# Closing a full expert in the gate logits on ScalarE, and making the repeated search keys on ScalarE alone

## The chip, the core and the metric

The kernel runs on one core of one Trainium2 chip. The metric is the device time of one execution in microseconds (us). Before the change the median of three runs is 2402.73 us (2402.56 to 2403.67).

## The reference: squared-ReLU attention, then experts filled greedily to capacity

```python
scores = scale * np.matmul(z, z.transpose(0, 2, 1))     # z: 8 x 2496 x 64
attn = np.maximum(scores, 0.0) ** 2
x = (u * np.matmul(attn, v)).reshape(B * S, D)          # 19968 x 256
logits = x @ w_gate                                     # 8 experts
for idx in np.argsort(-logits.flatten()):               # best logit first
    tok, e = idx // E, idx % E
    if assigned[tok] >= 0 or counts[e] >= cap:          # cap = 19968 / 8 = 2496
        continue
    assigned[tok] = e
    counts[e] += 1
for e in range(E):                                      # every expert on its 2496 tokens
    out[assigned == e] = np.maximum(x[assigned == e] @ w1[e], 0.0) @ w2[e]
```

A token goes to its best expert that still has room. An expert that is full is out of the race, and its remaining tokens go to their next best.

## The kernel before

The attention fills the first 1,360 us or so and isn't touched. After it, `moe` runs the experts one after the other, in the order in which they become full: k = 0 to 7. The tokens of an expert are worked on in five groups g of 512 (the last has 448), and each group in eight steps f. A step is 14 or so matmuls on TensorE (PE): six in `expand` (L664 to L666, into one of two PSUM buffers `hp`), and eight in `contract` (L757 and L760, for a step three earlier). Between them stand ScalarE's ReLU, which writes `hh` (L742), and VectorE's low half of the product, `hl_` (L744). For the last group VectorE also writes a piece of `hh` (L747), which is the last to read `hp`. A buffer `hp` is filled again only when ReLU, L744 and L747 have read it. VectorE also adds the outputs `y` (L784), splits weights (`w1l`, L613, behind ScalarE's `w1h`, L610) and turns gathered tokens (`tr`, L644).

While PE works on expert k-1, the generator `route(k)` finds the tokens of the next one. Its work is cut into pieces by `yield`, and `advance` hands out so many pieces per step. So the code's order mixes the two, and a scheduler at build time sets the final order on each engine from it; each engine then runs its own list in order. For k = 1 to 7 `route(k)` does this:

- It closes the expert that was filled last: `closed` (128 x 8) is a large negative number in its column and zero elsewhere, and is added to the logits `lg` (128 partitions x 160 tokens x 8 experts) on VectorE in two halves (L343). `closed` shares its memory with `rab`, which the one-hot rows of the expert before still read, so that it comes behind the last of them.
- `best_steps` (L81 to L98) finds each token's best expert and its logit `m`, in two halves.
- `order_keys` turns `m` into integer keys, and `spread` repeats their upper 16 bits eight times side by side in `rep` (L136 on ScalarE for the first half of the tokens, L137 on VectorE for the second).
- Two stages of six search rounds follow. A round compares `rep` with up to seven thresholds (`mask`, L128), counts on PE (L288, L399) and picks the next thresholds (L404, L408). Between the stages `spread` fills `rep` again, from `near`. The last expert needs no search.
- At the end it ranks the tokens (`tot`, L458 and L470, and what follows), makes one-hot rows `ob` in eight large instructions (L515), and PE turns these in four blocks (L521) into the list `idx` (L526), from which GpSimd gathers the tokens (L582).

The expert k = 0 has its own code and nothing of it changes.

Of the kernel before, what the change touches and what calls it, by code (L numbers as in the profile page):

```python
# [14 lines left out]
AF = mybir.ActivationFunctionType  # L15
# [60 lines left out]
def best_steps(nc, first, c, eq):  # L76
    lg, m, code, oh = [first[n][:, c] for n in ("lg", "m", "code", "oh")]
    shape = list(lg.shape)
    E = shape[2]
    cb = first["code8b"][:, None, :].to_broadcast(shape)  # L80
    nc.vector.tensor_reduce(m, lg, axis=AX.X, op=OP.max)  # L81
    yield
    nc.vector.tensor_tensor(eq, lg, m[:, :, None].to_broadcast(shape), op=OP.is_ge)
    yield
    nc.vector.tensor_mul(eq, eq, cb)
    yield
    if shape[1] < E:
        nc.vector.tensor_reduce(code, eq, axis=AX.X, op=OP.max)
        yield
        nc.vector.tensor_tensor(oh, code[:, :, None].to_broadcast(shape), cb, op=OP.is_equal)  # L90
        return
    nc.vector.tensor_max(eq[:, :, :4], eq[:, :, :4], eq[:, :, 4:])
    yield
    nc.vector.tensor_max(eq[:, :, :2], eq[:, :, :2], eq[:, :, 2:4])
    yield
    nc.vector.tensor_max(code, eq[:, :, 0], eq[:, :, 1])
    yield
    nc.vector.tensor_tensor(oh, code[:, :, None].to_broadcast(shape), cb, op=OP.is_equal)  # L98


def order_keys(nc, first, c, alone=False):
    for _ in key_steps(nc, first, c, alone):
        pass


def key_steps(nc, first, c, alone):
    m, sign, key, rep, top, low = [first[n][:, c] for n in ("m", "sign", "key", "rep", "top", "low")]
    m = m.bitcast(I32)
    nc.vector.tensor_scalar(sign, m, 31, 0x7FFFFFFF, op0=OP.arith_shift_right, op1=OP.bitwise_and)
    yield  # L110
    nc.vector.scalar_tensor_tensor(key, m, 0x8000, sign, op0=OP.bitwise_xor, op1=OP.bitwise_xor)
    yield
    half = key.bitcast(I16).rearrange("p (j h) -> p j h", h=2)
    spread(nc, rep, half[:, :, 1], alone)
    yield
    if half.shape[1] == first["key"].shape[1]:
        nc.scalar.activation(top, half[:, :, 1], AF.Copy, scale=65536.0)
        nc.scalar.activation(low, half[:, :, 0], AF.Copy)
        return
    nc.vector.tensor_scalar(top, half[:, :, 1], 65536.0, None, op0=OP.mult)  # L120
    yield
    nc.vector.tensor_copy(low, half[:, :, 0])


def at_least(nc, mask, x, T, lo, hi):
    for a in range(0, T.shape[1], 8):
        z = min(T.shape[1], a + 8)
        nc.vector.tensor_tensor(mask[:, lo:hi, a:z], x[:, lo:hi, :z - a],  # L128
                                T[:, None, a:z].to_broadcast([128, hi - lo, z - a]), op=OP.is_ge)


def spread(nc, rep, x, alone=False):
    n = x.shape[1]
    h = 0 if alone else n // 2
    if h:
        nc.scalar.activation(rep[:, :h], x[:, :h, None].to_broadcast([128, h, 8]), AF.Copy)  # L136
    nc.vector.tensor_copy(rep[:, h:], x[:, h:, None].to_broadcast([128, n - h, 8]))  # L137


def moe(tc, xd, first, jp, identf, w1, w2, out, B, S, cp, dram):  # L140
    nc = tc.nc
    E, D, F = w1.shape
# [7 lines left out]
    lg, m, code, oh, code8, code8b, xr = [first[n] for n in ("lg", "m", "code", "oh", "code8", "code8b", "rep")]  # L150
    JP = lg.shape[1]
# [14 lines left out]
    with ExitStack() as ctx:  # L166
# [109 lines left out]
        def srch():  # L276
            return ps.tile([128, 512], F32, name="srch", bufs=1)
# [56 lines left out]
        def behind(lag):  # L334
            return tc.issue_after(paced[-lag].ins) if len(paced) >= lag else nullcontext()

        def route(k):
            if k:
                closed = rp.tile([128, E], F32, name="closed", tag="rab")
                nc.vector.tensor_scalar(closed, ROUTE[k - 1]["star"], SHUT, None, op0=OP.mult)  # L340
                for c in range(0, JP, JP // 2):
                    o = lg[:, c:c + JP // 2]
                    nc.vector.tensor_add(o, o, closed[:, None, :].to_broadcast([128, JP // 2, E]))  # L343
                    yield 0.7
                for c in range(0, JP, JP // 2):
                    eq = rp.tile([128, JP // 2, E], BF, name="eq")
                    for i, _ in enumerate(best_steps(nc, first, slice(c, c + JP // 2), eq)):
                        if i == 2:
                            yield 6.8 / 4
                    yield 6.8 / 4  # L350
                done = rp.tile([128, JP], F32, name="done")
                with behind(1):
                    nc.vector.tensor_scalar(done, asg, 0.0, GONE, op0=OP.is_gt, op1=OP.mult)
                nc.vector.tensor_add(m, m, done)
                order_keys(nc, first, slice(0, JP))
                yield 1.5
# [13 lines left out]
            else:  # L370
# [7 lines left out]
                for stage in range(2):  # L378
                    for r, w in enumerate(widths):
                        n = (1 << w) - 1  # L380
                        if r == 0:
                            T = first["at0"] if k == stage == 0 else at0
                        else:
                            T = rp.tile([128, ND + 1], I16, name="T", bufs=2)[:, :n + 1]
                            nc.vector.tensor_tensor(T, step[:, r, :n + 1], V.to_broadcast([128, n + 1]), op=OP.add)
                        whole = first["mask0"] if n > 7 else rp.tile([128, JP, n], BF, name="mask")
                        cuts = [0, JP] if k else [JP - 16, JP] if T is first["at0"] else [0, JP // 2, JP]
                        for lo, hi in zip(cuts, cuts[1:]):
                            at_least(nc, whole, xr, T[:, :n], lo, hi)
                        yield 2  # L390
                        if k:
                            x = hist(lambda j: whole[:, j, :n], n, "jt")
                        else:
                            p, o = quad_hist(lambda j: whole[:, j, :n], n, r)
                        warm(k, 4)
                        yield 2.2
                        if k:
                            o = srch()[:, :E * (n + 1)]
                            nc.tensor.matmul(o, onesr, x, start=True, stop=True)  # L399
                        else:  # L400
                            quad_sums(p, o, n, "jt")
                        warm(k, 10 if r + 1 < len(widths) or stage else 30)
                        best = rp.tile([128, E, ND + 1], F32, name="best")[:, :, :n + 1]
                        nc.vector.scalar_tensor_tensor(best, o.rearrange("p (e t) -> p e t", e=E), 0.0,  # L404
                                                       T[:, None].to_broadcast([128, E, n + 1]),
                                                       op0=OP.min, op1=OP.add)
                        V = rp.tile([128, 1], F32, name="V", bufs=3)
                        nc.vector.tensor_reduce(V, best, axis=AX.XY, op=OP.max)  # L408
                    tstar = V
                    if stage == 0:  # L410
                        base = rp.tile([128, 1], F32, name="base")
                        nc.vector.tensor_scalar(base, tstar, 65536.0, None, op0=OP.mult)
                        rel = rp.tile([128, JP], F32, name="rel")
                        nc.vector.scalar_tensor_tensor(rel, first["top"], base, first["low"],
                                                       op0=OP.subtract, op1=OP.add)
                        near = rp.tile([128, JP], I16, name="near")
                        nc.vector.tensor_scalar(near, rel, 32767.0, -32768.0, op0=OP.min, op1=OP.max)
                        spread(nc, xr, near)
                        yield 1.5
                T = tstar  # L420
                g = rp.tile([128, 2, JP], BF, name="fmask")
# [4 lines left out]
                if k:  # L426
                    x = hist(lambda j: g[:, :, j], 2, "tj")
                    yield
                    o = srch()[:, :E * 2]
                    nc.tensor.matmul(o, onesr, x, start=True, stop=True)  # L430
                else:
                    p, o = quad_hist(lambda j: g[:, :, j], 2, 1)
# [3 lines left out]
                o = o.rearrange("p (e t) -> p e t", t=2)  # L436
# [63 lines left out]
            if k:  # L500
                p = srch()
                for c in range(0, JP, CB):
# [16 lines left out]
                    for j in range(c, min(J, c + CB)):  # L519
                        n, r = divmod(j - c, QW)  # L520
# [16 lines left out]
            for a0, a1 in ((0, 8), (8, 2 * KT)):  # L537
                na = a1 - a0
                p = srch()
                for c in range(0, JP, CB):  # L540
# [13 lines left out]
                    for j in range(c, min(J, c + CB)):  # L554
                        n, r = divmod(j - c, QW)
# [746 lines left out]
```

## Time and profile before

| what | value |
|---|---|
| median of the runs | 2402.73 us |
| the profiled execution: time | 2405.74 us |
| its span, first to last instruction | 2403.9 us |
| PE busy | 2367.9 us, 99% |
| VectorE (DVE) busy | 2026.1 us, 84% |
| ScalarE (ACT) busy | 1531.9 us, 64% |
| GpSimd (POOL) busy | 474.9 us, 20% |
| mean granted clock of PE | 0.995 |

Shares of the whole span say little about a single stage: VectorE is idle for a sixth of the span, and yet there are stretches in which it never stops. The time of the profiled execution lies 1.84 us over its span and 3.0 us over the median of the runs.

### The profile page before, as it was taken

How to read it: one execution, taken by the hardware profiler on the slowest of the kernel's cores; microseconds unless marked ns; L12 is line 12 of the kernel's file. 1: busy time of each engine (PE TensorE's matmuls, PEld its weight loads, DVE VectorE, ACT ScalarE, POOL GpSimd, SP SyncE). 2: the span in 40 equal slices, each digit the busy share in tenths (PEclk: the TensorE clock that was granted, in tenths of full speed). 3: DMA queues.
4: the chain of work that ended last, by engine and by line, in shares of the span. 5: the costliest groups of instructions: out<-in, count | busy, mean ns of one | idle time of the engine just before them, and what ended most of it. 6: DMA issues, size and time to landing. Idle time of an engine off the chain costs nothing.

```text
span 2403.9 us, 42413 instructions
## 1 busy us (share of the span) xinstructions
PE 2367.9 (99%) x14724; PEld 1985.2 (83%) x14724; DVE 2026.1 (84%) x5887; ACT 1531.9 (64%) x2932; POOL 474.9 (20%) x693
## 2 busy tenths in 40 slices
PE   8999999999999999999999999999999999999998
PEld 6888888888888888888888777788888888888887
DVE  7899898998999998999989888979797979797443
ACT  7898888988889888898888413424342434244332
POOL 3010020020010100200200013324333334344332
PEclk9999999999999999999999899999999999999999
DMA  4254262262262351622512112334342424243331
GB/s 150 49 134 102 53 157 53 58 178 50 52 161 53 83 145 34 160 75 54 138 27 53 27 54 80 110 84 123 82 123 81 128 79 132 78 141 105 101 98 54
DMA packets 233847, 222.27 MB, mean 92 GB/s; under 512 B 95392, under 2 KB 192672, under 8 KB 233504
## 3 DMA queue, kind: packets, MB, share of 16 engines
q1 hardware_dynamic: 193088, 150.58, 23.3%
q0 software_dynamic: 40544, 68.98, 10.5%
q8 instruction: 116, 1.90, 0.3%
q14 instruction: 99, 0.81, 0.1%
HBM read 158.67 MB, written 60.82 MB: 91 GB/s over the span
## 4 chain that ended last, share of the span: by engine, by line
PE 83%; issue 8%; DVE 4%; POOL 3%; DMA 1%; ACT 1%; POOLq 0%; DVEq 0%; SPq 0%; ACTq 0%
PE acc L1029 41%; PE sc L987 11%; PE y L757 8%; PE hp L664 4%; PE hp L665 4%; PE hp L666 4%; PE y L760 4%; POOL xg L582 2%; PE acc L1034 1%; PE srch L288 1%; POOL out_dram L792 1%; PE srch L521 1%; DMA zr<-in_z_dram 1%; PE xp L330 1%; DVE mask L128 1%
## 5 line engine op out<-in xcount | busy, mean ns | idle before, releaser
L1016 DVE TENSOR_TENSOR lo<-r,hi 128x512 fp32r<-128x512 f32 (+1 forms) x800 | 536.7, 674 | 82.1 <-ACT hi L1008 78.8
L1029 PE MATMUL acc<-hi,vh 128*128 128x512 f32 (+1 forms) x1520 | 591.3, 389 | 0.8 <-ACT vh L961 0.8
L1029 PE MATMUL acc<-lo,vh 128*128 128x512 f32 (+1 forms) x1520 | 588.2, 387 | 2.7 <-DVE lo L1016 2.7
L1029 PE MATMUL acc<-hi,vl 128*128 128x512 f32 (+1 forms) x1520 | 586.4, 386 | 0.0
L1008 ACT ACTIVATE hi<-r 128x512 fp32r<-128x512 f32 (+1 forms) x780 | 500.4, 642 | 122.3 <-ACT r L1003 86.1
L742 ACT ACTIVATE hh<-hp 128x512 fp32r<-128x512 f32 (+1 forms) x319 | 187.1, 587 | 557.0 <-PE hp L666 482.9
L1003 ACT ACTIVATE r<-r 128x512 f32<-128x512 f32 (+1 forms) x800 | 504.0, 640 | 2.5 <-DVE r L997 2.4
L1070 DVE SCALAR_TENSOR_TENSOR lt<-xs,wgb 128x256 bf16<-128x256 f32 x1192 | 449.7, 418 | 0.6 <-DMA xs<-xd 0.4
L757 PE MATMUL y<-w,hh 128*128 128x512 f32 x1280 | 367.1, 398 | 0.2 <-DVE y L784 0.2
L1029 PEld LDWEIGHTS acc<-hi,vh 128*128 128x128 f32 x1520 | 286.3, 188 | 67.0 <-issue 13.8
L999 ACT ACTIVATE r<-sc 128x512 f32<-128x512 f32 (+1 forms) x638 | 312.4, 617 | 40.2 <-PE sc L987 39.7
L1029 PEld LDWEIGHTS acc<-lo,vh 128*128 128x128 f32 x1520 | 286.5, 188 | 59.2 <-DVE lo L1016 8.5
L1029 PEld LDWEIGHTS acc<-hi,vl 128*128 128x128 f32 x1520 | 286.5, 188 | 51.9 <-DVE vl L971 0.2
L582 POOL DMA_INDIRECT xg<-xd,idx x160 | 186.8, 1168 | 465.0 <-DVE xg L620 269.0
L757 PEld LDWEIGHTS y<-w,hh 128*128 128x128 f32 x1280 | 235.5, 189 | 45.1 <-DVE y L784 1.3
L664 PE MATMUL hp<-xh,w1h 128*128 128x512 f32 (+2 forms) x642 | 255.9, 400 | 3.9 <-DVE hh L747 2.4
L665 PE MATMUL hp<-xl,w1h 128*128 128x512 f32 (+2 forms) x642 | 251.4, 392 | 0.6 <-DVE xl L658 0.5
L666 PE MATMUL hp<-xh,w1l 128*128 128x512 f32 (+2 forms) x642 | 249.8, 389 | 0.0
L987 PE MATMUL sc<-z,z 64*128 64x512 f32 (+1 forms) x1920 | 235.9, 388 | 5.3 <-ACT z L952 2.7
L987 PEld LDWEIGHTS sc<-z,z 64*128 64x128 f32 x1920 | 202.6, 185 | 29.6 <-ACT z L952 3.4
L792 POOL DMA_INDIRECT out_dram<-y,idx x160 | 169.0, 1056 | 215.0 <-DVE y L784 126.2
L950 POOL DMA_DIRECT2D z<-in_z_dram x35 | 18.7, 534 | 960.3 <-DVE lt L1070 639.6
(1192 smaller groups left out, 2880.9 us busy)
## 6 DMA issues: line engine op xcount, KB each, us to landing
ur<-in_u_dram SPq DMA_DIRECT2D x39, 512.0 KB, 4.6
flat<-tr SPq DMA_DIRECT2D x152, 128.0 KB, 2.8
xt<-flat SPq DMA_DIRECT2D x38, 512.0 KB, 3.6
vh<-in_v_dram POOLq DMA_DIRECT2D x133, 128.0 KB, 4.6
vr<-in_v_dram SPq DMA_DIRECT2D x32, 512.0 KB, 4.3
xd<-tr SPq DMA_DIRECT2D x128, 128.0 KB, 3.0
xs<-xd SPq DMA_DIRECT2D x32, 512.0 KB, 4.4
wr<-in_moe_w_dram SPq DMA_DIRECT2D x32, 512.0 KB, 5.9
```

The costliest lines, as they stand in the source:

```text
L582: return nc.gpsimd.indirect_dma_start(out=dst, out_offset=None, in_=src, in_offset=bass.IndirectOffsetOnAxis(ap=idx, axis=0))
L664: nc.tensor.matmul(p[:, c], wh, xh, start=(d == 0), stop=False)
L665: nc.tensor.matmul(p[:, c], wh, xl, start=False, stop=False)
L666: latest["mm"] = nc.tensor.matmul(p[:, c], wl, xh, start=False, stop=(d == DH - 1))
L757: nc.tensor.matmul(o, h[:, c], w.rearrange("p s d -> p (s d)"), start=(f == 0), stop=(f == FT - 1), skip_group_check=True)
L987: nc.tensor.matmul(pair[s], key[b, p][r, c * 128:c * 128 + 128], query[b, g][r, :w], start=key is ZH and query is ZH, stop=key is ZL)
L999: recent["r"] = nc.scalar.activation(r, p, AF.Relu, scale=scale)
L1003: nc.scalar.activation(R[n], R[n], AF.Square)
L1008: nc.scalar.activation(h, R[n], AF.Copy)
L1016: recent["l"] = nc.vector.tensor_sub(LO[n], a, h.bitcast(F32))
L1029: nc.tensor.matmul(o[d], w[:, c[d]], x, start=(kt == 0 and i == 0), stop=False)
L1070: nc.vector.scalar_tensor_tensor(t[r], src[r], 1.0, WG["rows"][r, e], op0=OP.mult, op1=OP.mult, accum_out=lg[r, j, e:e + 1])
```

## The change

For a full expert, ScalarE now adds `closed` to the logits, in eight instructions, one for each expert's column, each with that column of `closed` as its bias (`AF.Identity`). The two pieces that `advance` counted for it at 0.7 are now one of 1.4. And where `spread` filled half of `rep` on each engine, ScalarE fills all of it for the keys of k = 1 to 7 and for `near` of k = 1 to 6; VectorE's half goes away. The first expert, and the partial calls inside the attention, stay as they were.

```diff
     half = key.bitcast(I16).rearrange("p (j h) -> p j h", h=2)
-    spread(nc, rep, half[:, :, 1], alone)
+    n = half.shape[1]
+    spread(nc, rep, half[:, :, 1], 0 if alone else n if n == first["key"].shape[1] else n // 2)
     yield
-    if half.shape[1] == first["key"].shape[1]:
+    if n == first["key"].shape[1]:
...
-def spread(nc, rep, x, alone=False):
+def spread(nc, rep, x, h):
     n = x.shape[1]
-    h = 0 if alone else n // 2
     if h:
         nc.scalar.activation(rep[:, :h], x[:, :h, None].to_broadcast([128, h, 8]), AF.Copy)
-    nc.vector.tensor_copy(rep[:, h:], x[:, h:, None].to_broadcast([128, n - h, 8]))
+    if h < n:
+        nc.vector.tensor_copy(rep[:, h:], x[:, h:, None].to_broadcast([128, n - h, 8]))
...
                 nc.vector.tensor_scalar(closed, ROUTE[k - 1]["star"], SHUT, None, op0=OP.mult)
-                for c in range(0, JP, JP // 2):
-                    o = lg[:, c:c + JP // 2]
-                    nc.vector.tensor_add(o, o, closed[:, None, :].to_broadcast([128, JP // 2, E]))
-                    yield 0.7
+                for e in range(E):
+                    nc.scalar.activation(lg[:, :, e], lg[:, :, e], AF.Identity, bias=closed[:, e:e + 1])
+                yield 1.4
...
-                        spread(nc, xr, near)
+                        spread(nc, xr, near, JP if k else JP // 2)
```

The change also moves what it doesn't name. The lists of the engines are the same until the end of the first expert's routing; from there on the routing work stands at other places among the steps. Three places matter, all in the routing of the second expert (k = 1) and the start of the third's. In the rows the numbers behind a name tell buffers apart; those of the changed kernel are 4 to 10 higher for the same thing.

On PE, the matmul of `tot`, with which the ranking of expert 1 begins. Before:

```order
L757 MATMUL y_20455<-w_19154,hh 128x512
L760 MATMUL y_20455<-w_19154,hl__20312 128x256
L664 MATMUL hp<-xh_20234,w1h 128x512
L665 MATMUL hp<-xl_20235,w1h 128x512
L666 MATMUL hp<-xh_20234,w1l 128x512
L757 MATMUL y_20456<-w_19154,hh 128x512
L470 LDWEIGHTS tri
L470 MATMUL srch<-tot,tri 128x2
```

After the change:

```order
L666 MATMUL hp<-xh_20242,w1l 128x512
L757 MATMUL y_20459<-w_19154,hh 128x512
L757 MATMUL y_20460<-w_19154,hh 128x512
L757 MATMUL y_20461<-w_19154,hh 128x512
L470 LDWEIGHTS tri
L470 MATMUL srch<-tot,tri 128x2
L757 MATMUL y_20462<-w_19154,hh 128x512
L760 MATMUL y_20459<-w_19154,hl__20394 128x256
```

It moved behind 11 more matmuls of the experts' steps (378 of them stand ahead of it before, 389 after); the search rounds ahead of it moved back by 5 to 22.

On VectorE, the end of expert 1's list `idx`, with `closed` of the third expert's routing, which starts there. Before:

```order
L340 TENSOR_SCALAR closed<-star 128x8
L744 SCALAR_TENSOR_TENSOR hl__20808<-hp,hh 128x384
L343 TENSOR_TENSOR lg<-lg,closed 128x640
L525 COPY idl_f<-srch 128x20
L343 TENSOR_TENSOR lg<-lg,closed 128x640
L526 SCALAR_TENSOR_TENSOR idx<-srch,idl_f 128x20
L81 TENSOR_REDUCE m<-lg 128x80
L747 SCALAR_TENSOR_TENSOR hh<-hp,hh 128x64
```

After the change:

```order
L744 SCALAR_TENSOR_TENSOR hl__20818<-hp,hh 128x384
L341 TENSOR_SCALAR closed<-star 128x8
L747 SCALAR_TENSOR_TENSOR hh<-hp,hh 128x64
L784 TENSOR_TENSOR y<-y_20459,y 128x256
L784 TENSOR_TENSOR y<-y_20460,y 128x256
L525 COPY idl_f<-srch 128x20
L784 TENSOR_TENSOR y<-y_20461,y 128x256
L526 SCALAR_TENSOR_TENSOR idx<-srch,idl_f 128x20
L784 TENSOR_TENSOR y<-y_20462,y 128x256
L613 TENSOR_TENSOR w1l<-wr,w1h 128x512
L744 SCALAR_TENSOR_TENSOR hl__20861<-hp,hh 128x384
L81 TENSOR_REDUCE m<-lg 128x80
```

The two additions are gone, L747 moved ahead of `idx`, three `y` additions came ahead of it, and the first reduction of the logits stands behind `w1l`. On ScalarE the eight new instructions stand in one row, between the ReLU of the step before and `w1h`.

On VectorE again, some 25 instructions on: the low half of the step that PE reads next. Before:

```order
L98 TENSOR_TENSOR oh<-code,code8b 128x640
L354 TENSOR_TENSOR m<-m,done 128x160
L744 SCALAR_TENSOR_TENSOR hl__20924<-hp,hh 128x384
L109 TENSOR_SCALAR sign<-m 128x160
L747 SCALAR_TENSOR_TENSOR hh<-hp,hh 128x64
L111 SCALAR_TENSOR_TENSOR key<-m,sign 128x160
```

After the change:

```order
L109 TENSOR_SCALAR sign<-m 128x160
L96 TENSOR_TENSOR code<-eq 128x80
L111 SCALAR_TENSOR_TENSOR key<-m,sign 128x160
L98 TENSOR_TENSOR oh<-code,code8b 128x640
L744 SCALAR_TENSOR_TENSOR hl__20933<-hp,hh 128x384
L747 SCALAR_TENSOR_TENSOR hh<-hp,hh 128x64
```

The half (`hl__20924`, now `hl__20933`) has two more instructions of the third expert's routing ahead of it, `sign` and `key`.

## Rows read from the trace of the kernel before

**Rows 1.** The page: busy time of two engines, share of the span, instructions.
```profile
PE 2367.9 (99%) x14724; PEld 1985.2 (83%) x14724; DVE 2026.1 (84%) x5887; ACT 1531.9 (64%) x2932; POOL 474.9 (20%) x693
```
**Rows 2.** Busy time, instructions and granted clock (PEclk) in four stretches.
```profile
core 0: us, PE busy (x) PEld busy (x) DVE busy (x) ACT busy (x) POOL busy (x), PEclk, DMA share, GB/s
1505.00:1537.00 32.00, 28.91 (x282) 24.16 (x280) 31.72 (x64) 14.50 (x27) 5.01 (x5) 1.00 0.34 117
1537.20:1540.60 3.40, 3.40 (x11) 2.95 (x11) 3.40 (x10) 1.56 (x3) 2.49 (x4) 0.50 0.31 87
1540.60:1560.00 19.40, 17.83 (x104) 14.63 (x103) 19.21 (x53) 6.64 (x16) 10.14 (x10) 1.00 0.42 120
1562.00:2350.00 788.00, 786.29 (x5259) 663.33 (x5260) 608.35 (x1444) 281.91 (x549) 293.45 (x261) 1.00 0.36 104
```
**Rows 3.** Waits of PE, 1411 to 2404, first and last of nine: total, times, longest.
```profile
PE hp L664 <- DVE hh L747: 2.4, 1, 2.4
...
PE y L757 <- DVE y L784: 0.2, 1, 0.2
```
**Rows 4.** Timeline of PE, 1500 to 1550: start, duration, in brackets idle and releaser.
```profile
1508.73 0.18 PE L470 MATMUL srch<-tot,tri 128*128 128x2 bf16 x1
1533.45 1.08 PE L521 MATMUL srch<-hl,ob 128*128 128x40 f16 x36
1536.97 0.54 PE L664 MATMUL hp<-xh,w1h 128*128 128x448 f32 x1 [2.44 <-DVE hh L747]
1548.96 0.62 PE L760 MATMUL y<-w,hl__20924 128*128 128x256 f32 x3 [0.69 <-DVE hl__20924 L744]
```
**Rows 5.** Groups of instructions by shape, 1411 to 2404: busy, mean ns of one.
```profile
L343 DVE TENSOR_TENSOR lg<-lg,closed 128x640 f32<-128x640 f32 x14 | 11.1, 818 | 0.0
L137 DVE COPY rep<-key 128x640 int16<-128x640 int16 x7 | 3.4, 481 | 0.0
L137 DVE COPY rep<-near 128x640 int16<-128x640 int16 x6 | 3.0, 494 | 0.2
L742 ACT ACTIVATE hh<-hp 128x512 fp32r<-128x512 f32 x255 | 152.4, 598 | 482.7 <-PE hp L666 420.8 <-issue 25.8 <-PE srch L399 19.0
L509 ACT ACTIVATE hl<-oa,pcol 128x800 f16<-128x800 f16 x28 | 26.8, 957 | 18.3 <-DVE oa L506 11.2 <-PE srch L521 7.0
```
**Rows 6.** Timeline of ScalarE at the start of expert 1's routing.
```profile
1448.15 0.60 ACT L742 ACTIVATE hh<-hp 128x512 fp32r<-128x512 f32 x1 [2.17 <-PE hp L666]
1449.74 0.74 ACT L136 ACTIVATE rep<-key 128x640 int16<-128x640 int16 x1 [0.99 <-DVE key L111]
1450.39 0.32 ACT L117 ACTIVATE top<-key 128x160 f32<-128x160 int16 x1
1450.62 0.32 ACT L118 ACTIVATE low<-key 128x160 f32<-128x160 int16 x1
```
**Rows 7.** Timeline of VectorE, 1508 to 1549, single instructions.
```profile
1508.27 0.15 DVE L458 CAST tot<-cum 128x2 bf16<-128x2 f32 x1
...
1508.48 0.74 DVE L784 TENSOR_TENSOR y<-y,y 128x256 f32<-128x256 f32 x2
...
1531.70 1.48 DVE L515 TENSOR_TENSOR ob<-rab,slot 128x2560 f16<-128x2560 f16 x1
1533.11 0.68 DVE L613 TENSOR_TENSOR w1l<-wr,w1h 128x512 fp32r<-128x512 f32 x1
...
1535.80 0.16 DVE L526 SCALAR_TENSOR_TENSOR idx<-srch,idl_f 128x20 int32<-128x20 f32 x1
...
1536.62 0.21 DVE L747 SCALAR_TENSOR_TENSOR hh<-hp,hh 128x64 fp32r<-128x64 f32 x1
...
1548.37 0.54 DVE L744 SCALAR_TENSOR_TENSOR hl__20924<-hp,hh 128x384 fp32r<-128x384 f32 x1
1548.84 0.22 DVE L109 TENSOR_SCALAR sign<-m 128x160 int32<-128x160 int32 x1
```
**Rows 8.** Timeline of ScalarE: the split of the next first-layer weight.
```profile
1539.04 0.63 ACT L610 ACTIVATE w1h<-wr 128x512 fp32r<-128x512 f32 x1 [4.79 <-PE hp L665]
```
## The prediction

> **What bounds the kernel now.** First the page's busy times: PE works for 2367.9 us of the span of 2403.9, DVE for 84% and ACT for 64% [rows 1]. An edit that only unloads DVE can therefore gain no more than PE's own idle time and the time that PE runs at a lower clock. Next, stretch by stretch [rows 2]: from 1562 to 2350 us, where six of the seven changed routings lie, PE is busy for 786.29 of 788.00 us. There is nothing to gain there, only something to lose. From 1505 to 1560, where the second expert's routing (k = 1) ends and the next begins, it is otherwise: DVE is busy for 31.72 of 32 us and then for 19.21 of 19.4, and PE has gaps. So there DVE is the bound.
>
> The waits of PE after the attention are nine rows, from one of 2.4 us to one of 0.2 [rows 3]; the seven between are 1.0, 0.7, 0.6, 0.6, 0.5, 0.5 and 0.3, together 6.8 us. The timeline gives the two that count a place [rows 4]: at 1536.97 PE has stood 2.44 us for `hh` of L747, and at 1548.96 0.69 us for the low half `hl__20924`. Right behind the first the granted clock is 0.50 for 3.4 us [rows 2], that is 1.2 instead of 2.4 GHz, and a matmul of 448 columns takes 0.54 us: 1.7 us more are lost. The most that the change can gain after the attention is thus 6.8 + 1.7 = 8.5 us; realistically it is the two waits and the clock, 2.44 + 0.69 + 1.7 = 4.8.
>
> **The change part by part.** *The closing on DVE* goes: 14 additions of 818 ns [rows 5], 11.1 us in seven places, 1.5 us each after overlap. *The second halves of `rep`* go from DVE too: 3.4 + 3.0 us [rows 5]. DVE is thus relieved of 17.5 us. In six of seven routings this is worth nothing, since PE never waits for DVE there. What hides it is PE's own queue of steps.
>
> *The closing on ACT* has no row before. From below: an activation over 128x160 without a per-partition operand takes 0.32 us, and the next starts 0.23 later [rows 6]. The plain rows, 0.32 us at 160 elements and 598 ns at 512 [rows 5, 6], give 0.79 ns for an element and so 0.83 us at 800; the row with a per-partition operand, 128x800, takes 957 ns [rows 5], 0.13 more. A part of that may be its other type; I take 0.09 for the operand. So 0.41 us for one, 0.32 us from start to start, eight in 2.6 us; bounds 1.9 (spacing 0.23) and 3.3 (8 x 0.41). The Trainium skill, "ScalarE: Activation LUTs", section "Rules for kernel authors", gives about 0.3 us for an instruction with a pointer as bias and 0.83 ns for an element, which would be an estimate of 0.43 us each; no run here shows the form yet.
>
> So a closing takes ACT about 1.1 us longer than DVE, and by that the first reduction of the logits can begin later. *`rep` on ACT*: the half took 0.74 us [rows 6] and ran beside DVE's 0.48. The whole takes at most 2 x 0.74 = 1.48 and at least 0.74 if it were all fixed cost; I take 1.28. It delays each first mask by some 0.55 us, 13 times. PE has main work queued there, and a delay of the routing costs nothing as long as its list comes before its gather is needed, so I take nothing for it (bound: 13 x 0.55 = 7 us if every mask were waited for).
>
> *What moves.* On PE the matmul of `tot` stands 11 main matmuls later. Main matmuls follow each other by 0.22 us on average (eight experts of five groups of eight steps of 14 are 4480 in the 993 us from 1411 to 2404 us, the routing's matmuls between them taken in), so the ranking of expert 1 starts 11 x 0.22 = 2.4 us later; I take 2.3: at 1511.0 instead of 1508.7 [rows 4]. From `tot` on, 1508.27, until the last half of `ob` is done at 1533.18, DVE is never idle and the chain is a list of DVE work of 24.9 us [rows 7]. Of this list three `y` additions (0.37 each, 0.74 for two [rows 7], so 1.0 in overlap) and one low half (0.54) have already been done when `tot` is later, and one `w1l` (0.68 [rows 7]) comes in: 24.9 - 1.0 - 0.6 + 0.6 = 23.9. So `ob` ends at 1511.0 + 23.9 = 1534.9 instead of 1533.2. PE reaches its last L521 block where it did, at 1533.5 [rows 4], waits some 1.3 us, and ends it near 1536.0. Now the order helps: L747 stands ahead of `idx`, hence directly behind `ob`, so `hp` is free at about 1535.8 and PE goes on at 1536.0 to 1536.2, against 1536.97. That is 0.8 to 1.0 gained.
>
> `idx` ends near 1536.9 (before 1535.96, from 1535.80 [rows 7]): the `y` additions are ahead of it. From there DVE's list to the low half that PE reads next took 1535.96 to 1548.91, 12.9 us [rows 7]. Now three `y` additions have gone ahead (-1.0) and `sign` and `key` have come ahead of it (+0.4, `sign` 0.22 [rows 7]): 12.3 us of work. But one instruction in this list now waits. `w1l` stands ahead of the first reduction, and needs ACT's `w1h`; ACT could write that only from 1539.04 on, after PE's last use of the old weight (a wait of 4.79 us for PE at L665 [rows 8]), and now the eight closings stand in its queue ahead of it. DVE's `y` additions last until about 1537.8, `w1h` is done at 1539.7: some 1.9 us in which DVE is idle for the first time in this stretch, with `m`, the keys and the low half behind it in its queue. So the low half comes at 1536.9 + 12.3 + 1.9 = 1551.1, with `hl__20933` in its name now, and PE at about 1551.2, against 1548.96: +2.3. PE arrives there about 0.9 us earlier than its 1548.27, or, if the half clock of 1537 goes away, up to 2.6: I take 1547, a wait of 4.2 us. Behind a wait of that length I expect the half clock again, as it came behind that of 2.44; half of the 1.7 us, 0.85, adds to the end, for the routing's matmuls in it aren't late. Against it two later waits of the seven go, 0.4 for a mask and 0.3 for `xh`, as PE is late for both. Sum: +2.3 + 0.85 - 0.7 = +2.45, and 0.15 for a gather that is waited for a little longer, +2.6 us. On the profiled execution, span 2403.9 and 1.84 around it (2405.7, itself 3.0 over the median), this is 2408.3; on the median, 2402.7 + 2.6 = **2405.3 us**.
>
> **The rivals.** A is the sum above, 0.50; its own range is 2403.5 (the low half only 0.8 us late) to 2407.5 (half clock in full, closings at 3.3).
>
> B, faster: the two additions (1.5 us) and VectorE's spread are off DVE where it is the bound, ACT is idle enough there (14.50 of 32 us, then 6.64 of 19.4 [rows 2]) to have closed the logits in time, and `w1l` finds its `w1h` ready. It decides if the low half is done before PE comes at 1547; then the wait of 2.44 and the clock's 1.7 are gone, -4.1, 2398.6. Against it speaks the later `tot`. Chance 0.12.
>
> C, no change: some other stall of the same size takes the place of the 2.44 and the 0.69, PE's work being the same, so 2402.7, give or take 1. Chance 0.20.
>
> D, clearly slower: ACT is the neck at each of the seven closings. Eight in a row, up to 8 x 0.41 = 3.3 us, stand ahead of the ReLU that frees `hp`. A step takes 993 / 320 = 3.1 us (1411 to 2404, eight experts of five groups of eight steps), `hp` is needed again about one and a half steps after it is full, 4.6 us, and ReLU (0.60 [rows 5]) and the low half (0.54 [rows 7]) take 1.1 of it: a slack of 3.5 us less what ACT is already behind. From the third expert on the changed order puts other ACT work among the eight, so that at most six stand in a row, and the slack about holds. Where it doesn't, PE loses 0.5 to 1 us at each of seven: +6, 2409. The same page and section as above says to use VectorE and not ScalarE for an addition; by that rule alone this would be the outcome, as the closing takes 2.6 us instead of 1.5, and the trace so far bears out the longer time but not that anyone waits for it. Chance 0.18.
>
> **How the numbers follow.** A measurement of this kernel tells 0.2%, 4.8 us, from no change: faster is below 2397.9, slower above 2407.5. A puts little above 2407.5, 0.05 of its 0.50, and nothing below; B's 2398.6 lies on the near side of the bound, about half of its 0.12 below it; C is all the same; D nearly all slower, 0.17. So faster 0.06, same 0.72, slower 0.22. The range leaves out the lower half of B and the upper half of D: 2399.5 to 2409.0.
>
> **What would show it.** DVE's busy time falls by about 17.5 us, ACT's rises by 56 x 0.41 + 13 x 0.55 = 30. `tot` stands near 1511; PE waits about 1.3 us ahead of the last L521 block; L747 ends before `idx`; DVE is idle for nearly 2 us ahead of `w1l`; PE waits over 3 us for `hl__20933`, with half clock behind it; from 1562 on PE still idles for no more than 2 us. The prediction is wrong if `w1h` comes early (then B), or if ACT's closing takes over 3.4 us and PE shows waits for ReLU at every expert's start (then D).

## The result, and the profile after

The changed kernel takes 2416.49 us (median of four runs, 2414.6 to 2418.23), against 2402.64 in the same comparison: a ratio of 1.0053, interval 1.0041 to 1.0065. It is slower by 13.9 us, clearly outside the forecast range. Its profiled execution took 2414.6 us, the least of the four, span 2412.7. Repeated on another chip it came to 1.0047 (1.0034 to 1.0061).

The attention varies from execution to execution by some microseconds, and the profiles share that. I therefore count from the first `closed` on VectorE, where the change begins, to the end of the span. Before, `closed` starts at 1435.36 and 968.5 us follow. After, it starts at 1432.91 and 979.8 follow: 11.3 us more, where the two spans differ by 8.8 only.

The page's busy times, engines as in [rows 1]:

```profile
PE 2366.8 (98%) x14724; PEld 1981.7 (82%) x14724; DVE 2013.2 (83%) x5860; ACT 1567.0 (65%) x2988; POOL 472.5 (20%) x693
```

VectorE has 12.9 us less, where 17.5 were forecast, and ScalarE 35.1 more. The groups by shape, as in [rows 5], tell why it is more than the 30 forecast:

```profile
L343 ACT ACTIVATE lg<-lg,closed 128x160 f32<-128x160 f32 x56 | 29.7, 627 | 5.1 <-DVE closed L341 5.1
L81 DVE TENSOR_REDUCE m<-lg 128x80 f32<-128x640 f32 x14 | 11.4, 816 | 11.7 <-ACT lg L343 11.7
...
L136 ACT ACTIVATE rep<-key 128x1280 int16<-128x1280 int16 x7 | 8.9, 1271 | 9.0 <-DVE key L111 9.0
L136 ACT ACTIVATE rep<-near 128x1280 int16<-128x1280 int16 x6 | 7.6, 1263 | 2.0 <-DVE near L417 2.0
```

One of the eight instructions of a closing takes 627 ns, not 410; the whole `rep` takes 1.27, as forecast. And VectorE stands 11.7 us, over the seven starts, for ScalarE's closings. The waits of PE from 1411 us on, where before had [rows 3]:

```profile
PE y L760 <- DVE hl__20933 L744: 6.9, 1, 6.9
PE srch L521 <- DVE ob L515: 2.9, 2, 1.9
PE hp L664 <- DVE hh L747: 2.5, 2, 1.5
PE y L757 <- DVE y L784: 2.5, 4, 0.6
```

The timeline of PE puts them in place; the rows of 1510, 1535, 1541 and 1554 answer to [rows 4]:

```profile
1442.09 0.50 PE L664 MATMUL hp<-xh,w1h 128*128 128x512 f32 x1 [0.84 <-DVE hl__19536 L744]
...
1510.58 0.18 PE L470 MATMUL srch<-tot,tri 128*128 128x2 bf16 x1
...
1519.90 1.19 PE L521 MATMUL srch<-hl,ob 128*128 128x40 f16 x40 [1.87 <-DVE ob L515]
...
1535.57 1.08 PE L521 MATMUL srch<-hl,ob 128*128 128x40 f16 x36 [1.03 <-DVE ob L515]
...
1541.48 0.44 PE L664 MATMUL hp<-xh,w1h 128*128 128x448 f32 x1 [0.94 <-DVE hh L747]
...
1554.37 0.58 PE L760 MATMUL y<-w,hl__20933 128*128 128x256 f32 x1 [6.93 <-DVE hl__20933 L744]
...
1670.10 0.44 PE L664 MATMUL hp<-xh,w1h 128*128 128x448 f32 x1 [1.52 <-DVE hh L747]
...
1793.52 1.04 PE L757 MATMUL y<-w,hh 128*128 128x512 f32 x2 [0.60 <-DVE y L784]
```

The wait of 2.44 us for `hh` is gone from its place, as forecast, though two new ones for `hh`, of 0.94 and 1.52 us, stand elsewhere. The large wait is for the low half that was named, but it is 6.93 us long. The granted clock behind the wait of 1.87 us and behind that of 6.93, columns as in [rows 2]:

```profile
1519.90:1527.90 8.00, 8.00 (x110) 7.03 (x111) 8.00 (x11) 3.47 (x5) 0.00 (x0) 1.00 0.21 68
1554.40:1557.60 3.20, 3.20 (x17) 2.68 (x18) 3.20 (x11) 0.47 (x3) 0.00 (x0) 0.53 0.45 156
```

VectorE around it, as in [rows 7]:

```profile
1510.26 0.17 DVE L458 CAST tot<-cum 128x2 bf16<-128x2 f32 x1
...
1514.31 0.69 DVE L613 TENSOR_TENSOR w1l<-wr,w1h 128x512 fp32r<-128x512 f32 x1 [1.02 <-ACT w1h L610]
...
1534.04 1.48 DVE L515 TENSOR_TENSOR ob<-rab,slot 128x2560 f16<-128x2560 f16 x1
...
1537.19 0.17 DVE L526 SCALAR_TENSOR_TENSOR idx<-srch,idl_f 128x20 int32<-128x20 f32 x1
...
1537.61 0.68 DVE L613 TENSOR_TENSOR w1l<-wr,w1h 128x512 fp32r<-128x512 f32 x1
...
1540.39 0.82 DVE L81 TENSOR_REDUCE m<-lg 128x80 f32<-128x640 f32 x1 [1.64 <-ACT lg L343]
...
1548.00 1.25 DVE L644 STREAM_TRANSPOSE tr<-xg 128x1024 f32<-128x1024 f32 x1 [2.95 <-DMA xg<-xd,idx]
...
1553.77 0.55 DVE L744 SCALAR_TENSOR_TENSOR hl__20933<-hp,hh 128x384 fp32r<-128x384 f32 x1
```

From `idx` (done at 1537.36) to the low half (done at 1554.32) lie 17.0 us. 1.64 of them are a wait for the closings, 2.95 a wait for gathered tokens, and the other 12.4 are the list that was forecast at 12.3. Why the tokens are late stands on GpSimd's timeline, in the order of its queue:

```profile
1536.80 0.97 POOL L792 DMA_INDIRECT out_dram<-y,idx  x1 [25.07 <-DVE y L784]
1538.07 1.06 POOL L792 DMA_INDIRECT out_dram<-y,idx  x1 [0.30 <-issue]
1539.44 0.97 POOL L792 DMA_INDIRECT out_dram<-y,idx  x1 [0.31 <-issue]
1540.71 0.99 POOL L582 DMA_INDIRECT xg<-xd,idx  x1 [0.30 <-issue]
```

Three output scatters stand ahead of the gather. Before, the gather was first, 4.5 us earlier on the clock:

```profile
1536.24 0.99 POOL L582 DMA_INDIRECT xg<-xd,idx  x1 [24.09 <-DVE idx L526]
```

ScalarE's timeline shows the closings at the first and the second start; the eight are one row, 0.53 us from start to start:

```profile
1433.99 4.13 ACT L343 ACTIVATE lg<-lg,closed 128x160 f32<-128x160 f32 x8
1438.03 0.57 ACT L742 ACTIVATE hh<-hp 128x512 fp32r<-128x512 f32 x1
1439.09 0.60 ACT L742 ACTIVATE hh<-hp 128x512 fp32r<-128x512 f32 x1 [0.49 <-PE hp L666]
...
1536.10 4.26 ACT L343 ACTIVATE lg<-lg,closed 128x160 f32<-128x160 f32 x8 [0.92 <-DVE closed L341]
1540.21 0.66 ACT L610 ACTIVATE w1h<-wr 128x512 fp32r<-128x512 f32 x1
```

At the first start VectorE stands behind them with its first reduction, and the low half for which PE waits 0.84 us at 1442.09 comes three routing steps later:

```profile
1438.15 0.82 DVE L81 TENSOR_REDUCE m<-lg 128x80 f32<-128x640 f32 x1 [3.34 <-ACT lg L343]
...
1441.35 0.68 DVE L744 SCALAR_TENSOR_TENSOR hl__19536<-hp,hh 128x512 fp32r<-128x512 f32 x1
```

### The profile page after: what moved, and what is told of

Read it like the earlier page. It is cut to its first block, busy times and chain, and to the rows that moved or that the text cites. A ratio compares the mean times of both kernels' runs of the same rounds, so it can differ in the third digit from the quotient of the medians.

```text
span 2412.7 us, 42430 instructions
## 1 busy us (share of the span) xinstructions
PE 2366.8 (98%) x14724; PEld 1981.7 (82%) x14724; DVE 2013.2 (83%) x5860; ACT 1567.0 (65%) x2988; POOL 472.5 (20%) x693
## 4 chain that ended last, share of the span: by engine, by line
PE 77%; issue 9%; DVE 6%; POOL 3%; ACT 2%; DMA 1%; SPq 0%; POOLq 0%; DVEq 0%; ACTq 0%
PE acc L1029 40%; PE sc L987 11%; PE y L757 7%; PE hp L664 4%; PE hp L665 4%; PE hp L666 4%; PE y L760 3%; POOL xg L582 2%; PE srch L289 1%; PE acc L1034 1%; POOL out_dram L792 1%; ACT lg L343 1%; PE xp L331 1%; DVE lo L1016 1%; DVE mask L129 1%
```

## The experiments

The ratio in each is to the kernel before, run beside it on the same chip. The table below divides the profiled executions: lag against before, counted from the first `closed`, at two ReLUs that are the same work in every kernel (the 291st and the 271st from the end; before, at 1517.88 and 1586.10 us) and at the end. "List" is what is lost between the two, where the second list is made, "later" what is lost after. "Place" is by how many main matmuls `tot` stands later on PE than before. There is one profile of before, from the first comparison. Where a kernel has nothing changed, its parts agree with that within 0.1 us (e7 up to the end of the list, e12 outside it). e10 and e11 have no such first `closed`, and on the chip of e13 to e15 PE waited in new places; these five are not in the table.

| kernel | place | start | list | later | all |
|---|---|---|---|---|---|
| the change | +11 | 0.8 | 6.9 | 3.5 | 11.3 |
| e1, closings only | -7 | 1.5 | 0.6 | 5.4 | 7.5 |
| e2, keys only | -7 | -0.3 | -0.1 | 0.1 | -0.3 |
| e3, third closing back | +11 | 1.3 | 4.6 | 3.7 | 9.6 |
| e4, gather first | +11 | 1.1 | 6.2 | 3.5 | 10.7 |
| e5, routing earlier | -9 | 1.3 | 1.7 | 4.4 | 7.3 |
| e6, before, routing later | +6 | 0.4 | 2.5 | -0.6 | 2.3 |
| e7, before, closings k > 2 | 0 | 0.0 | 0.1 | 5.2 | 5.2 |
| e9, one column on ScalarE | -7 | 0.3 | 0.7 | -1.3 | -0.3 |
| e12, before, gather late | 0 | 0.0 | 7.1 | 0.0 | 7.0 |

**e1: the closings alone.** `spread` as before.

```diff
-                for c in range(0, JP, JP // 2):
-                    o = lg[:, c:c + JP // 2]
-                    nc.vector.tensor_add(o, o, closed[:, None, :].to_broadcast([128, JP // 2, E]))
-                    yield 0.7
+                for e in range(E):
+                    nc.scalar.activation(lg[:, :, e], lg[:, :, e], AF.Identity, bias=closed[:, e:e + 1])
+                yield 1.4
```

> Closings on ScalarE, the repeated keys as before. Theory C (the closing is the loss: eight instructions of 0.53 us each, at the second list's end and at the five later starts): 2409 to 2416 us, with 4 or more waits of 0.6 us of PE for the output additions after 1600 us. Theory S (the repeated keys are the loss, since the masks come later and the ranking's matmul stands later on PE): 2401 to 2405 us.

Measured 2413.25 us, ratio 1.0038 (1.0023 to 1.0052). The waits of 0.6 us for the output additions are there, and the later starts cost 5.4 us. Theory C holds for these, and S falls. But C names the second list's end too, and there e1 loses 0.6 us where the change loses 6.9: with the keys as before, `tot` stands 7 matmuls earlier than in the kernel before, and not 11 later. So by the profiles most of the list's loss comes only with both edits together, through the order that they give.

**e2: the keys alone.** All edits of `spread`, the closings as before.

```diff
...
-                        spread(nc, xr, near)
+                        spread(nc, xr, near, JP if k else JP // 2)
```

> Repeated keys on ScalarE alone, closings on VectorE as before. Theory C: 2401 to 2405 us, no change, and no waits for the output additions. Theory S: 2408 us or more.

Measured 2404.36 us, ratio 0.9999 (0.9989 to 1.0009): no difference that the runs can tell.

**e3: the change with the third expert's closing on VectorE.**

```diff
+                if k != 2:
                     for e in range(E):
                         nc.scalar.activation(lg[:, :, e], lg[:, :, e], AF.Identity, bias=closed[:, e:e + 1])
                     yield 1.4
+                else:
+                    ...
```

> The change, but the closing for the third expert's routing (k = 2) stays on VectorE. Theory C: the stall of 6.9 us in front of the low half falls to that of before, and the five later starts keep their 0.6 us and more each: 2405 to 2409 us. Theory T (the later ranking matmul alone makes the second list late): the stall stays at 3 us or more, 2411 us or more.

Measured 2414.53 us, ratio 1.0040 (1.0026 to 1.0054). The stall of 6.9 falls to one of 1.4 and one of 1.3, yet the time by the end is as theory T has it. 4.6 of the 6.9 us of the list stay without this closing; they are now waits for the one-hot rows, the low halves and an output addition (1.0 us):

```profile
PE srch L527 <- DVE ob L521: 3.4, 2, 2.3
```

Theory C alone does not explain the second list.

**e4: the gather first.** The scatters of the group ahead are held behind the gather; only GpSimd's list differs from the change.

```diff
...
+                with tc.issue_after(LASTG[1, 0].ins) if (k, g) == (0, NG - 2) else nullcontext():
                     st = nc.gpsimd.indirect_dma_start(
```

> The change, but the gather of the second expert's first tokens is held ahead of the three output scatters on GpSimd's queue; the lists of the other engines are the same row for row. Theory G (VectorE's turn of the gathered tokens waits 2.95 us for this gather, and the low half stands behind it): the stall of 6.9 us falls to about 4, 2412 to 2414.5 us. If the closing alone sets it: the stall stays over 6 us, 2415 to 2418 us.

Measured 2414.87 us, ratio 1.0040 (1.0026 to 1.0055). The turn of the tokens no longer waits and the stall is 2.8 us shorter:

```profile
PE y L761 <- DVE hl__20933 L745: 4.1, 1, 4.1
```

The table shows a gain of only 0.7 in the list, because this execution lost 4.06 us to the lower clock, the change 1.5 (PE's busy time by the share of the clock not granted, summed over stretches of 1 us from 1400 on): here the wait for one-hot rows was 2.1 us, not 1.87, and half clock followed it from 1521 on. PE's row, and the stretch behind it:

```profile
1521.48 1.43 PE L521 MATMUL srch<-hl,ob 128*128 128x40 f16 x40 [2.10 <-DVE ob L515]
1521.90:1525.10 3.20, 3.20 (x37) 2.72 (x34) 3.09 (x5) 0.96 (x1) 0.00 (x0) 0.50 0.44 164
```

The intervals of the two ratios overlap, so that the runs alone do not tell e4 from the change; the shorter stall is the profile's.

**e5 and e6: the place of `tot`.** e5 is the change, e6 is the kernel before; both move only the point at which the second expert's routing begins.

```diff
-        starts = [None, 2 * (AHEAD + 2), 2 * (PER + LATE)] + [2 * PER * k for k in range(2, E)]
+        starts = [None, 2 * (AHEAD + 1) + 1, 2 * (PER + LATE)] + [2 * PER * k for k in range(2, E)]
```

In e6 the second number is `2 * (AHEAD + 4)`.

> The whole change, with the second expert's routing begun one half step earlier in the code, which puts its ranking matmul back to where it stood or ahead of it (357 main matmuls of the steps ahead by a count that leaves out the first buffers, where before has 366 and the change 377). Theory T (the later ranking matmul is what makes the second list late): the loss of some 7 us between 1518 and 1586 falls to under 2, the whole to 5 to 7 us above before. Theory C (the closing alone, wherever it stands): 9 us or more above before.

Measured 2410.1 us, ratio 1.0028 (1.0018 to 1.0039). The list's loss falls from 6.9 to 1.7. The waits for the one-hot rows are gone; one of 3.8 for the low half stays:

```profile
PE y L760 <- DVE hl__20933 L744: 3.8, 1, 3.8
PE y L757 <- DVE y L784: 2.4, 4, 0.6
```

> The kernel before, with the second expert's routing begun two steps later in the code, so that its ranking matmul stands 6 main matmuls later and the one-hot blocks nearly where the change has them; closings and repeated keys untouched. Theory T: 3 to 5 us above before, with new waits for the one-hot rows. Theory C: within 1 us of before.

Measured 2406.22 us, ratio 1.0007 (0.9998 to 1.0017). Its profile loses 2.5 us in the list, of which 1.35 are clock (3.06 against 1.71); the runs do not tell it from nothing. The expected waits for one-hot rows did not come. So six places alone cost little, and theory T is not borne out here; the change and e5, twenty places apart and both with the closings on ScalarE, differ by 5.2 us in the list.

**e7: closings on ScalarE from the fourth routing on.** The kernel before, with a condition as in e3, here `k > 2`.

> Closings on ScalarE only from the fourth expert's routing on (k = 3 to 7), all else as before. Theory C at the later starts (0.6 us and 1.5 us of wait at each): 3 to 5 us above before, and all of it after 1650 us. If the later starts are slower for another reason: within 1 us of before.

Measured 2409.01 us, ratio 1.0021 (1.0011 to 1.0030), all of it after 1650:

```profile
PE y L762 <- DVE y L789: 2.5, 4, 0.7
```

**e8: the price.** Twelve activations that change no value, in the kernel before; `null` is a column of zeros, and `flat` the logits read contiguously.

```diff
+                    for i in range(3):
+                        nc.scalar.activation(lg[:, :, i], lg[:, :, i], AF.Identity, bias=null)
+                    for i in range(3):
+                        nc.scalar.activation(lg[:, :, i], lg[:, :, i], AF.Copy)
+                    for i in range(3):
+                        c = flat[:, 160 * i:160 * i + 160]
+                        nc.scalar.activation(c, c, AF.Identity, bias=null)
+                    for i in range(3):
+                        c = flat[:, 160 * i:160 * i + 160]
+                        nc.scalar.activation(c, c, AF.Copy)
```

> The kernel before, with twelve activations that change no value in the fifth expert's routing: 128x160 in place, three each with stride 8 and a column as bias, with stride 8 and none, contiguous with a bias, contiguous without. If the stride is what makes a closing cost 0.53 us: the contiguous forms cost some 0.32 to 0.41 and the strided ones 0.5 to 0.6, bias or not. If the bias does: the two with a bias cost over 0.5, the others 0.32. If it is that each reads what the one before wrote nearby: all four cost the same.

The groups of ScalarE by shape (the whole execution took 2402.86 us):

```profile
L350 ACT ACTIVATE lg<-lg,null 128x160 f32<-128x160 f32 x3 | 1.7, 622 | 0.2 <-DVE lg L343 0.2
L352 ACT ACTIVATE lg<-lg 128x160 f32<-128x160 f32 x3 | 1.5, 549 | 0.0
L355 ACT ACTIVATE lg<-lg,null 128x160 f32<-128x160 f32 x3 | 1.1, 420 | 0.0
L358 ACT ACTIVATE lg<-lg 128x160 f32<-128x160 f32 x3 | 0.8, 322 | 0.0
```

The bias column adds 73 to 98 ns, as I had priced it; the stride of eight elements adds 202 to 227. It is the stride.

**e9: one column on ScalarE.** The change, but only the full expert's column is closed, found by a register; `closed` is a column that holds the large negative number.

```diff
-                for e in range(E):
-                    nc.scalar.activation(lg[:, :, e], lg[:, :, e], AF.Identity, bias=closed[:, e:e + 1])
+                at = nc.scalar.value_load(ROUTE[k - 1]["which"], min_val=0, max_val=E - 1)
+                o = lg[:, :, bass.ds(at, 1)]
+                nc.scalar.activation(o, o, AF.Identity, bias=closed)
```

> The whole change, but ScalarE closes only the column of the expert that is full, found by a register that it loads: one instruction of 0.6 us in place of eight (4.2 us), all else as in the change. Theory C (the 4.2 us ahead of the first reduction are the loss): within 2 us of before, with no waits for the output additions at the later starts. If a closing on ScalarE costs wherever and however short it is (a hand-over between engines): 4 us or more above before.

Measured 2405.12 us, ratio 0.9996 (0.9986 to 1.0005), and no wait for an output addition of 0.2 us or more. ScalarE's group:

```profile
L344 ACT ACTIVATE lg<-lg,closed x7 | 4.4, 624 | 3.9 <-DVE closed L341 3.9
```

Seven such instructions on ScalarE cost nothing that the runs can tell. `tot` stands 7 matmuls earlier here and not 11 later, so the fair comparison is e5, which has 56 of them, the keys on ScalarE and `tot` 9 earlier: 7.3 us by the profile against -0.3 here.

**e10 and e11: one column on VectorE.** The kernel before, and the same with the keys on ScalarE.

```diff
...
+                at = nc.vector.value_load(ROUTE[k - 1]["which"], min_val=0, max_val=E - 1)
+                o = lg[:, :, bass.ds(at, 1)]
+                nc.vector.tensor_scalar(o, o, SHUT, None, op0=OP.add)
```

> The kernel before, with VectorE closing only the column of the full expert through a register: one instruction of some 0.3 us in place of two of 0.8. VectorE's list behind the second list is 1.3 us shorter less the load: if that list sets the wait of 2.4 us for hh, it falls to 1.0 to 1.7, 1 to 3 us below before. If the load of the register costs as much as the addition saved: within 0.5 us of before.

> As the run before with VectorE's one column, and the repeated keys on ScalarE alone: the same as that run within 1 us, as the spread moved nothing by itself; if VectorE's second halves of the keys count in the full stretch, 0.5 to 1.5 us less.

Measured 2409.81 (1.0018, 1.0008 to 1.0027) and 2411.49 us (1.0024, 1.0015 to 1.0034): slower, against both theories. Without the tile `closed`, nothing held the second expert's closing behind the first expert's one-hot rows any more, and it stands in the middle of that list:

```profile
1401.86 0.31 DVE L341 TENSOR_SCALAR lg<-lg  x1 [1.71 <-issue]
```

VectorE stood 1.71 us ahead of it, in which its queue loads the register (547 ns) and works out the address; the first reductions followed it there, and PE waited 3.6 us for that list's last rows, with half clock behind (8.45 us lost). Those rows are from e10. e11 shows the same wait of 3.6 us, with 8.3 us lost behind it; its median is 1.7 us above that of e10, so that its expectation, the same or less, failed too.

**e12: the gather late in the kernel before.** Only GpSimd's list differs: four scatters stand ahead of the gather.

```diff
+            with tc.issue_after(scat[-2]) if (k, g) == (1, 0) else nullcontext():
                 for i in range(4):
                     gather(t[:, i], xd, idx[:, 4 * g + i:4 * g + i + 1])
...
```

The part left out moves the gather one step later in the code.

> The kernel before, with the gather of the second expert's first tokens held behind four output scatters on GpSimd's queue; the lists of all other engines are the same row for row. Theory G (VectorE's turn waits for the gather, and the low half behind it makes PE wait): VectorE idle for 4 to 5 us ahead of the turn, the wait of 0.7 us of PE for the low half becomes 4 to 6, 4 to 6 us above before. If VectorE's list has slack there: within 1 us of before.

Measured 2412.67 us, ratio 1.0029 (1.0018 to 1.0040); VectorE, then PE:

```profile
1550.44 1.25 DVE L645 STREAM_TRANSPOSE tr<-xg 128x1024 f32<-128x1024 f32 x1 [5.49 <-issue]
```

```profile
1554.32 1.01 PE L761 MATMUL y<-w,hl__20924 128*128 128x256 f32 x3 [6.25 <-DVE hl__20924 L745]
```

VectorE's list has no slack for a late gather here: 7.1 us in the list, 1.5 of them clock (3.21 lost against 1.71).

**e13 and e14: one column on VectorE from the third routing on**, the second closing as before; e14 with the keys on ScalarE too.

> The kernel before, with VectorE closing one column through a register from the third expert's routing on (k = 2 to 7); the second expert's closing stays as it was, so that no load of the register can stand in the first expert's list (in the run with it at all seven, that list's last rows came 3.6 us late and PE ran at half clock behind it, 8.45 us; from there to the end that run then gained 5.8 us). If these 5.8 us are the shorter list: 2 to 6 us below before. If they only made up for the delay: within 1 us of before.

> As the run before, with the repeated keys on ScalarE alone: within 1.5 us of that run.

Measured 2406.51 us, ratio 0.9986 (0.9977 to 0.9995), and 2406.74, ratio 0.9988 (0.9979 to 0.9997), on a chip on which before took 2409.28. The two are the fastest versions, 2.5 to 2.8 us below before, and the runs do not tell them apart. In the profile of e13 the wait for `hh` is 2.1 us and no half clock follows it:

```profile
PE hp L671 <- DVE hh L754: 2.1, 1, 2.1
```

**e15: the change again**, beside e13 and e14.

> The change itself once more, beside the others on one chip: 1.0041 to 1.0065 of before, 11 us from the first closing to the end above before by the profile, of these 6 to 7 between 1518 and 1586.

Measured 2420.46 us, ratio 1.0047 (1.0034 to 1.0061), with the same stall:

```profile
PE y L760 <- DVE hl__20933 L744: 6.9, 1, 6.9
```

By the ratio this is as expected. By its profile it is not: set against the profile of before from the other chip, it loses 17.0 us from the first `closed` on, 8.3 of them in the list, where 11 and 6 to 7 were expected. On this chip PE also waited in new places in all three kernels (for `hx`, in the search rounds), and no profile of before was taken there, so how much of this is the chip's stays open.

## Why the prediction was wrong, point by point

**The places were mostly right, the sizes were not.** The wait for `hh` went from its place, PE waited ahead of the last one-hot block (1.03 us, forecast 1.3), VectorE stood still ahead of the first reduction (1.64, forecast 1.9), the big wait was for `hl__20933`, and half clock followed it (1.5 us lost). The forecast of +2.6 lies wholly in the list, between 1518 and 1586 us. The profile has 11.3: 0.8 ahead of the list and 3.5 behind it, where the forecast has nothing, and 6.9 in it. So one half of the 8.7 us that were missed is a term put at nothing, and the other half is a list that came later than was summed.

**The term put at nothing is the later reduction at six of the seven starts.** The prediction has a closing 1.1 us longer on ScalarE, "and by that the first reduction of the logits can begin later", and charges this in the list alone. For the rest stand "What hides it is PE's own queue of steps" and, under D, "the slack about holds"; the first start, at 1433 us, is in no sum. The slack did not hold. VectorE stood at the first reduction of every start, 3.34 us at the first, 2.08 at the fourth expert's and 0.7 to 1.3 at the last four, and the low halves and output additions behind it in VectorE's list came later. PE waited 0.84 us at the first start, 1.52 for `hh` at the fourth expert's and four times 0.6 for the output additions. e7 has the later starts alone, 5.2 us in its profile, and e9, with one instruction in place of eight, has none of these waits. Not all of it shows as idle time: PE idles 5.0 us in e7 from 1562 to 2389 us and 1.7 before from 1562 to 2385, which is 3.3 of the 5.2. Where the other 1.9 go stays open.

**The price behind it was wrong too**: "So 0.41 us for one, 0.32 us from start to start, eight in 2.6 us; bounds 1.9 (spacing 0.23) and 3.3". The rows that it was read from are contiguous; 0.42 is what a contiguous one with a bias does cost. An instruction of a closing writes every eighth element, and costs 0.62, eight in 4.13 and 4.26 us, beyond the upper bound. Whether eight in 2.6 us would have cost PE as much, no run tells. The Trainium skill, page "ScalarE: Activation LUTs", section "Rules for kernel authors", says to use VectorE and not ScalarE for an addition. The runs agree for the eight strided ones, which take 4.2 us on ScalarE where the two on VectorE took 1.5; seven single ones on ScalarE cost nothing (e9), and the reason that the Trainium skill gives, VectorE's rate for an element in bf16, is not what ran here. The figures of the same section of the Trainium skill (0.43 us as the estimate) fit the contiguous row of e8 with 0.42, not the closing's 0.62.

**Rival D was near in size**, at chance 0.18: +6, with 4.3 measured outside the list. Its path was another. A ReLU did stand behind the eight at the first start. But the ReLU that the late low half `hl__19536` needs was done at 1439.69, and the low half began at 1441.35: it stood behind VectorE's routing steps, and these behind the closings. In the changed kernel's list of waits none is for a ReLU.

**"From `tot` on"**: counted from the first `closed`, `tot` was 4.4 us later (1510.26 - 1432.91 against 1508.27 - 1435.36), not 2.3. That it stood near the forecast 1511 was luck, as this execution was 2.5 us ahead at its first `closed`. The searches ahead of it were late too, behind the closing of the first start. And the list behind it took 25.3 us, not 23.9: VectorE waited 1.02 there for the `w1h` of the `w1l` that moved in, and of the three `y` additions that the sum takes out only two had stood in that list ([rows 7] show them). So `idx` was 3.8 us late, not 0.9. The runs support that this place carries most of the list's loss: with the routing earlier (e5) 6.9 becomes 1.7, without the third closing (e3) only 4.6. They do not show it alone: six places in the kernel before (e6) cost little.

**"One instruction in this list now waits"**: one did, but for the closings and not for `w1h`. The `w1l` of 1537.61 does not wait at all; the `w1h` of 1540.21 is not its own. The rows of before told this: there the `w1l` in that place starts while the `w1h` of [rows 8] is still being written (until 1539.67).

```profile
1539.21 0.67 DVE L613 TENSOR_TENSOR w1l<-wr,w1h 128x512 fp32r<-128x512 f32 x1
```

The size, 1.64 against 1.9, came out by luck.

**What was left out is GpSimd's queue.** I counted the three `y` additions as moved ahead of `idx`, on VectorE, and not that each releases an output scatter that the gather then follows. That is 2.95 us of the 6.93. e4 takes it out of the wait, and e12, where VectorE waits 5.49 us for the gather, loses 7.1 us in the list of the kernel before with nothing else changed. Together: counted from the first `closed`, the low half came 7.9 us later than before, where 2.2 were forecast, and the 5.7 between are 2.9 of `idx` and 2.95 of the gather, less 0.2 in the rest.

**Where hiding was claimed it held for the keys** (e2). **Rival B** kept a part: with the additions off VectorE at little cost from the third routing on (e13), the kernel gains 2.8 us, of the 4.1 that B forecast, and no half clock follows its wait for `hh`. What the 2.8 us are made of isn't shown, for the same want of a profile of before from that chip. ScalarE in eight strided pieces was the wrong place.

## What to carry to other kernels

Price an instruction by a row with its access pattern, not only its shape and operands: a column out of eight is no contiguous row. When the order of one engine moves, follow what each moved instruction releases into the in-order queues of the others, the DMA issuer's first. And before work is moved to an idle engine, ask whether it can shrink: here seven of the eight columns were added zero.

## What the runs showed of the hardware

ScalarE's 128x160 in place takes 322 ns contiguous and 549 with a stride of eight 4-byte elements, 420 and 622 with a bias column. A wait of PE of 1.87 us was followed by the full clock in the change; one of 2.10 at the same place in e4 by half of it (1.65 us lost). The length of the wait alone does not decide: one of 2.08 us for `hh` left the clock full in e10 and was followed by half of it in e11. The stretches behind these two, e10 first:

```profile
1544.80:1550.80 6.00, 6.00 (x31) 5.30 (x32) 6.00 (x15) 2.24 (x4) 4.50 (x5) 1.00 0.30 87
1544.50:1547.50 3.00, 3.00 (x10) 2.47 (x9) 3.00 (x8) 1.69 (x3) 2.18 (x3) 0.50 0.33 100
```

Chips differ: the same kernel before had medians from 2402.6 to 2409.3 us in the comparisons here, which is more than most effects in this study.
